# Fewer fills of the score tiles on GpSimd, and a later load of one small column

## The chip, the cores and the metric

The kernel runs on one core of a Trainium2 chip. The metric is the device time of one execution in microseconds; the median of three runs is used. The core has five engines that run their own instruction queues in order and wait for each other by semaphores: TensorE (PE; its weight loads are shown as PEld), VectorE (DVE), ScalarE (ACT), GpSimd (POOL) and SyncE (SP), which here only issues DMA transfers.

## The reference

Gated linear attention over 4 batches, 8 heads, 768 steps and a head width of 48, all in fp32, and then a normalised MLP block on rows of 8 x 48 = 384:

```python
for t in range(S):
    state = alpha[:, :, t, :, None] * state + np.einsum('bhd,bhe->bhde', k[:, :, t], v[:, :, t])
    y[:, :, t] = np.einsum('bhd,bhde->bhe', q[:, :, t], state)
x = y.transpose(0, 2, 1, 3).reshape(B, S, H * D)
...
xn = (x - mu) / np.sqrt(var + 1e-06) * g_ln
out = x + np.maximum(xn @ w_ch1, 0.0) @ w_ch2
```

`w_ch1` is 384 x 1536 and `w_ch2` 1536 x 384. Both reach the chip as 64-bit words and are turned into fp32 there.

## The kernel before

The 768 steps are cut into 6 chunks of 128 steps; a chunk of one batch is one call of the generator `attention(c, b)`. In a chunk the recurrence becomes products: cumulated logarithms of alpha (ACT `la` L293, PE `lps` L298 for chunk 0 and L525 later), their exponentials times q and k (ACT L303 and L304, DVE `qk` L312), transposes (`tps` L328, copied to `qT` and `kT` by L333 and L335), scores (`aps` L369), and then `yps`, which sums scores times v (L424). `ups` (L399) and the DVE product L408 carry the state on.

Chunk 0 (`whole`) is done as one block of 128 x 128 scores for each head: ACT copies the scores from PSUM to an SBUF tile `at` (L379), and POOL clears what lies on the wrong side of the diagonal by an affine select (L380). Two tiles `at` of 128 x 1024 serve four batches in turn, so the selects are four for the batches 0 and 1 and four for the batches 3 and 2. All later chunks are done in two halves of 64 steps, and there DVE writes the scores by a predicated copy (L383) that writes only the positions that count. It relies on zeros standing in the others. POOL therefore fills both tiles with zeros at the start (L278) and again when chunk 0 has read them for the last time (L462). A half of an `at` tile then holds the scores of a batch.

The normalised rows `xn` (DVE L479) are transposed (`xps` L490). For chunk 0, DVE multiplies them by the column `g_col` of g on the way to `xT` (L493); for the later chunks g is multiplied into the weights instead (ACT L782, first at 65.9 us). `g_col` is a slice of the tile `small`, of 128 x 3 elements, and is loaded by a DMA that POOL issues (L310). All other DMA transfers are issued by SP: the inputs (`ra`, `rq`, `rk`, `vn`; L143, L147, L149, L160), the rows that carry the gates (`row` L316, `gate` L389), and the weight pieces `ws` (L211).

A weight piece is unpacked from 64-bit words by DVE (L223, L225, L227), ACT (L229), and DVE again (L231, L233). The first piece lets the hidden products of chunk 0 start (`hps` L564 on PE).

The order on every engine is the order of the program's text, and that is written out by hand: `ORDER` is a string in which each letter advances one generator by one step (`a` to `x` the attention of one chunk and batch, `A` on the weight pieces, `0` to `3` the loads, `Y`, `Z`, `M` and `V` the MLP's products, and so on). Constants are made on POOL first, in the tile `consts`: the triangle `tri` (L176, L177), the identity (L179, L180), the masks of halves (L182, L185) and a bf16 identity of halves (L189).

Of the kernel before, what the change touches and what calls it, by code (L numbers as in the profile page):

```python
# [51 lines left out]
def kernel(  # L52
# [36 lines left out]
    nc = tc.nc  # L89
# [4 lines left out]
    P = 128  # L94
# [18 lines left out]
    HS = P // 2  # L113
# [79 lines left out]
    small = cpool.tile([P, NF + 2], FP32, name="small")  # L193
    g_col, eps, least = small[:, :NF], small[:, NF:NF + 1], small[:, NF + 1:NF + 2]
# [79 lines left out]


    ats = [cpool.tile([P, NP, 2, 2, HS], FP32, name=f"at{i}") for i in range(2)]
    for at in ats:
        nc.gpsimd.memset(at, 0.0)  # L278

    x_of, xT_of, hT_of, las, lps_of, qkT_of, aps_of, ob_of = ({} for _ in range(8))  # L280

# [2 lines left out]
    def attention(c, b):  # L284
# [20 lines left out]
        yield  # L305
        ends = slice(P - 1, P) if whole else slice(HS - 1, P, HS)
        ne = 1 if whole else 2
        if c == b == 0:
            with nc.allow_non_contiguous_dma(reason="one small column load"):
                nc.gpsimd.dma_start(g_col, g_ln.rearrange("(f p) -> p f", p=P))  # L310
        for n in (0, 1) if whole else (1, 0):
            nc.vector.tensor_mul(qk[:, n], raws.pop(("qk"[n], c, b)), (eq, lv)[n])  # L312
            if n == 0:
# [4 lines left out]
        at = ats[b % len(ats) if whole else 1 - b % 2]  # L318
        if not whole:
            at = at.rearrange("k p i s t -> k (p i s t)")[:, b // 2 * NP * P:][:, :NP * P].rearrange(  # L320
                "k (p s t) -> k p s t", s=2, t=HS)
# [54 lines left out]
        if whole:  # L376
            for i in range(2):
                to = at[:, :, i].rearrange("k p s t -> k p (s t)")
                nc.scalar.copy(out=to, in_=aps[i].rearrange("k p s t -> k p (s t)"))  # L379
                nc.gpsimd.affine_select(out=to, in_=to, compare_op=AOP.is_ge, fill=0.0, base=0,  # L380
                                        pattern=[[0, NP], [1, P]], channel_multiplier=-1)
        else:
            nc.vector.copy_predicated(  # L383
                out=at.rearrange("k p s t -> k (p s) t"),
                data=aps[0].rearrange("k p s t -> k (p s) t"),
                mask=mask_of_halves.unsqueeze(1).broadcast_to([P, 2 * NP, HS]))
# [72 lines left out]
                nc.vector.scalar_tensor_tensor(out=x, in0=yps[1], scalar=1.0, in1=x, op0=AOP.mult,  # L459
                                               op1=AOP.add, accum_out=mean)  # L460
        if whole and b + len(ats) >= B:
            nc.gpsimd.memset(at, 0.0)  # L462
        yield
        if not whole:
            x_of[c, b] = kept = dram.tile([P, DM], FP32, name="kept", tag="kept", bufs=4 * B)
# [467 lines left out]
    turns |= {"PQ"[h]: second_of_chunk_0(h) for h in range(2)}  # L933
    turns |= {"4": sums(), "5": scores()}
    turns |= {chr(ord("a") + n): attention(n // B, n % B) for n in range(NCB * B)}
    turns |= {chr(ord("A") + i): take_weights(i) for i in range(len(pieces))}
    turns |= {"M": mlp(), "V": hidden_products(NCB - 1), "S": combine_first(), "W": combine_weights(), "R": relus(),
# [34 lines left out]
```

## Time and profile before

| | |
|---|---|
| median of three runs | 423.36 us (423.02 to 423.86) |
| the profiled execution's own time | 425.22 us |
| its span on the core | 423.5 us |
| instructions in the profile | 14142 |
| granted TensorE clock | full speed in all slices |
| DMA | 43.95 MB, 104 GB/s mean over the span |

The profile is of one execution. Times in it are microseconds from the start of the span unless marked ns. A line such as `start us, us, engine line op out<-in` gives the start, the length, the engine, the line of the kernel, and in brackets how long the engine had been idle before and what ended that; `x4` merges four instructions of a kind. In the chain of work that ended last each step is what released the next one.

### The profile page before, as it was taken

The page shows a single profiled execution, that of the slowest core. Times are in us where ns is not written, and L with a number is a line of the kernel's source. Part 1 is how long each engine was busy: PE and PEld are TensorE (multiplying, and loading weights), DVE is VectorE, ACT ScalarE, POOL GpSimd, SP SyncE. Part 2 cuts the span into 40 slices and gives each one's busy share as a digit, 9 for nine tenths or more (in the row PEclk, how much of TensorE's full clock was granted, in tenths as well). Part 3 has the DMA queues.
Part 4 walks back from the last instruction along what each step waited for, and adds up shares of the span by engine and source line. Part 5 has one row for each costly group of instructions (what it writes and reads, how often), then busy time and mean ns, then how long its engine had stood idle before and what let it go on. Part 6 is the DMA issues. An engine that isn't in the chain of part 4 may idle for free.

```text
span 423.5 us, 14142 instructions
## 1 busy us (share of the span) xinstructions
PE 416.0 (98%) x5988; PEld 366.6 (87%) x5988; DVE 326.9 (77%) x626; ACT 228.0 (54%) x572; POOL 155.2 (37%) x182
## 2 busy tenths in 40 slices
PE   7989999999999999999999999999999999999996
PEld 5878878756778889998889998899998899988996
DVE  3689989898998989778668667749676588756684
ACT  6987577969535879434666066496432541124300
POOL 4242010200116391244671334670145650656414
PEclk9999999999999999999999999999999999999999
DMA  7879866774533341161503136002122000130001
GB/s 234 242 210 276 259 180 187 229 224 146 115 109 122 97 147 45 38 180 30 150 23 111 61 90 159 0 22 39 42 82 70 0 2 0 39 112 2 0 20 56
DMA packets 50791, 43.95 MB, mean 104 GB/s; under 512 B 23164, under 2 KB 46844, under 8 KB 50728
## 3 DMA queue, kind: packets, MB, share of 16 engines
q1 hardware_dynamic: 50696, 43.04, 35.3%
q8 instruction: 47, 0.77, 0.8%
q14 instruction: 16, 0.13, 0.1%
q0 software_dynamic: 32, 0.00, 0.0%
HBM read 34.29 MB, written 8.74 MB: 102 GB/s over the span
## 4 chain that ended last, share of the span: by engine, by line
PE 91%; DVE 3%; DMA 3%; ACT 1%; issue 1%; SPq 1%; DVEq 0%
PE ops L676 31%; PE hps L856 31%; PE ops L576 7%; PE hps L564 7%; PE yps L440 5%; PE aps L541 2%; PE ups L399 2%; PE tps L349 2%; DMA ws<-in_moe_w_ch_dram 2%; PE lps L525 1%; DMA ra<-in_alpha_dram 1%; DVE qk L312 1%; PE xps L506 1%; PE tps L328 1%; PE xps L490 1%
## 5 line engine op out<-in xcount | busy, mean ns | idle before, releaser
L692 POOL TENSOR_TENSOR ob<-ob,u 128x192 f32<-128x192 f32 x40 | 25.5, 648 | 88.5 <-DVE ob L689 66.1
L856 PE MATMUL hps<-sum,w 128*128 128x256 f32 x192 | 47.5, 382 | 0.1
L414 POOL TENSOR_TENSOR mid<-mid,gate 112x192 f32<-112x192 f32 x20 | 10.7, 536 | 92.3 <-DVE mid L412 55.2
L856 PEld LDWEIGHTS hps<-sum,w 128*128 128x128 f32 x192 | 36.1, 190 | 5.1 <-DVE qk L312 0.2
L676 PE MATMUL ops<-w,hT 128*128 128x192 f32 x224 | 39.9, 327 | 0.0
L676 PEld LDWEIGHTS ops<-w,hT 128*128 128x128 f32 x224 | 37.0, 190 | 0.3
L564 PE MATMUL hps<-xT,w 128*128 128x256 f32 x144 | 33.6, 385 | 1.1 <-DVE w L233 0.8
L856 PE MATMUL hps<-xT,w 128*128 128x256 f32 x136 | 34.4, 380 | 0.0
L564 PEld LDWEIGHTS hps<-xT,w 128*128 128x128 f32 x144 | 26.5, 190 | 6.6 <-issue 1.1
L576 PE MATMUL ops<-w,hT 128*128 128x384 f32 x96 | 32.0, 488 | 0.0
L907 ACT ACTIVATE hT<-hT 128x512 f32<-128x512 f32 x48 | 27.3, 629 | 7.8 <-POOL hT L894 2.7
L856 PEld LDWEIGHTS hps<-xT,w 128*128 128x128 f32 x136 | 25.8, 190 | 3.5
L676 PE MATMUL ops<-ws,sum 128*128 128x192 f32 x160 | 28.6, 327 | 0.0
L576 PEld LDWEIGHTS ops<-w,hT 128*128 128x128 f32 x96 | 17.9, 190 | 11.5
L686 DVE TENSOR_TENSOR ob<-ops,ob 128x192 f32<-128x192 f32 x50 | 17.0, 351 | 13.0 <-PE ops L676 7.6
L676 PEld LDWEIGHTS ops<-ws,sum 128*128 128x128 f32 x160 | 26.4, 190 | 0.0
L359 ACT COPY qT<-tps 112x512 uint16<-112x512 uint16 x32 | 17.2, 600 | 16.0 <-PE tps L349 16.0
L676 PE MATMUL ops<-ws,hT 128*128 128x192 f32 x128 | 23.4, 326 | 0.0
L510 ACT COPY xT<-xps 128x384 uint16<-128x384 uint16 x32 | 13.5, 491 | 16.9 <-PE xps L506 16.9
L676 PE MATMUL ops<-more,sum 128*128 128x192 f32 x120 | 22.2, 328 | 0.0
L676 PEld LDWEIGHTS ops<-ws,hT 128*128 128x128 f32 x128 | 21.3, 190 | 0.1
L440 PE MATMUL yps<-mid,qT 48*64 48x48 f32 x320 | 20.9, 220 | 0.0
(254 smaller groups left out, 1138.0 us busy)
## 6 DMA issues: line engine op xcount, KB each, us to landing
ws<-in_moe_w_ch_dram SPq DMA_DIRECT2D x12, 768.0 KB, 5.9
vn<-in_v_dram SPq DMA_DIRECT2D x12, 384.0 KB, 3.9
kept<-x SPq DMA_DIRECT2D x20, 192.0 KB, 2.7
ob<-kept SPq DMA_DIRECT2D x20, 192.0 KB, 2.2
out_dram<-ob SPq DMA_DIRECT2D x19, 192.0 KB, 1.9
rq<-in_q_dram SPq DMA_DIRECT2D x16, 192.0 KB, 4.1
rk<-in_k_dram SPq DMA_DIRECT2D x16, 192.0 KB, 4.3
ra<-in_alpha_dram SPq DMA_DIRECT2D x14, 192.0 KB, 2.5
```

What stands on the lines that cost most here:

```text
L349: nc.tensor.transpose(tv[cs, n, p, w], words[halves[h], n, p, i, :cs.stop - cs.start, w], ident_of_halves[halves[h]])
L359: nc.scalar.copy(out=to, in_=tps[h].bitcast(UINT16).rearrange("r (n p w t) -> r n p t w", n=2, p=NP, w=2)[:R, n])
L414: nc.gpsimd.tensor_mul(new, new, by)
L440: nc.tensor.matmul(yps[r][halves[s], i, p], of, by, start=not (odd and inner), stop=bool(inner or not odd), skip_group_check=bool(odd))
L510: nc.scalar.copy(out=xT_of[c][:, :, b, halves[h]].bitcast(UINT16).rearrange("r f (t w) -> r f t w", w=2), in_=xps[h].bitcast(UINT16)[:, :2 ...
L564: nc.tensor.matmul(hps, w1[:, j // 2, f, j % 2 * P:][:, :P], xT_of[0][:, f, bs], start=(f == 0), stop=(f == NF - 1))
L576: nc.tensor.matmul(ops_of[b], hT_of[c][:, j, b], w2[:, j], start=(j == 0), stop=(j == NJ - 1))
L676: nc.tensor.matmul(acc, lhs[:, j], rhs[:, j], start=(j == 0), stop=(j == NT - 1))
L686: nc.vector.tensor_add(x, acc, x)
L692: getattr(nc.gpsimd, f"tensor_{op}")(x, x, y)
L856: nc.tensor.matmul(acc[:, i], w, b, start=True, stop=True)
L907: nc.scalar.activation(out=x, in_=x, func=AFT.Relu)
```

## The change

Three edits, all in what POOL does in the first 30 us. The fills of both `at` tiles at the start go. The fill behind chunk 0 is limited to the rows 0 to 63 and the second half of the columns of each block, a quarter of the tile: the select of chunk 0 leaves zeros in all other positions that the later chunks rely on. The load of `g_col` moves from the middle of the first call of `attention` to behind the second select of batch 1. The quantity that is computed stays the same.

```diff
     ats = [cpool.tile([P, NP, 2, 2, HS], FP32, name=f"at{i}") for i in range(2)]
-    for at in ats:
-        nc.gpsimd.memset(at, 0.0)
...
         ne = 1 if whole else 2
-        if c == b == 0:
-            with nc.allow_non_contiguous_dma(reason="one small column load"):
-                nc.gpsimd.dma_start(g_col, g_ln.rearrange("(f p) -> p f", p=P))
...
                 nc.gpsimd.affine_select(out=to, in_=to, compare_op=AOP.is_ge, fill=0.0, base=0,
                                         pattern=[[0, NP], [1, P]], channel_multiplier=-1)
+            if b == 1:
+                with nc.allow_non_contiguous_dma(reason="one small column load"):
+                    nc.gpsimd.dma_start(g_col, g_ln.rearrange("(f p) -> p f", p=P))
...
         if whole and b + len(ats) >= B:
-            nc.gpsimd.memset(at, 0.0)
+            nc.gpsimd.memset(at[:HS, :, :, 1], 0.0)
```

In the built program POOL's order changes as written, and the two casts of L189 come to stand ahead of the two selects of L185. The order of the instructions on all other engines stays as it was. Two copies L379 of ACT no longer wait for POOL, and POOL's first select L380 waits for POOL's own earlier work as well.

## The prediction

> **What bounds the kernel now.** First the page: busy shares, and the chain of work that ended last.
>
> ```profile
> PE 416.0 (98%) x5988; PEld 366.6 (87%) x5988; DVE 326.9 (77%) x626; ACT 228.0 (54%) x572; POOL 155.2 (37%) x182
> ```
>
> TensorE is busy for 416.0 of 423.5 us and the chain runs 91% over it; POOL has 37% and no share of the chain. So work taken from POOL is worth something only where TensorE waits behind POOL, and all that the change touches lies in the first 30 us. There I read the chain in order of time.
>
> ```profile
> 15.79 0.36 DVE st L408
> ...
> 18.05 7.05 DMA ws<-in_moe_w_ch_dram
> ...
> 30.48 2.83 PE hps L564 x12
> ```
>
> The head runs: loads of alpha (landing to 6.23), the first scores and products on PE (11.09 to 15.76), the state on DVE, the issue of the first weight piece at 18.05, its landing at 25.10, its unpacking on DVE and ACT, and at 30.48 the first hidden products. What moves a step of this moves the end almost one for one. Next POOL alone, in order of time:
>
> ```profile
> 3.22 0.51 POOL L189 CAST consts<-consts 64x64 bf16<-64x64 f32 x2
> 3.79 0.95 POOL L278 MEMSET at<- 128x1024 f32 x1
> 4.68 0.94 POOL L310 DMA_DIRECT2D small<-in_moe_g_ln_dram  x1
> 12.98 2.39 POOL L380 TENSOR_SCALAR_AFFINE_SELECT at<-at 128x512 f32<-128x512 f32 x4 [7.36 <-ACT at L379]
> 21.87 2.67 POOL L380 TENSOR_SCALAR_AFFINE_SELECT at<-at 128x512 f32<-128x512 f32 x4 [6.49 <-ACT at L379]
> 27.29 1.88 POOL L462 MEMSET at<- 128x1024 f32 x2 [2.76 <-PE yps L424]
> ```
>
> The first column is the start, the second the length. POOL stands idle for 7.36 us ahead of the first four selects, for 6.49 us ahead of the next four, and 4.06 us after the last fills (L414 follows at 33.24). Then DVE, which reads what POOL makes:
>
> ```profile
> 9.79 0.55 DVE L312 TENSOR_TENSOR qk<-rk,lps 128x384 f32<-128x384 f32 x1 [0.86 <-DMA rk<-in_k_dram]
> ...
> 22.79 0.54 DVE L493 TENSOR_TENSOR xT<-xps,small 128x384 f32<-128x384 f32 x1
> 23.57 0.56 DVE L493 TENSOR_TENSOR xT<-xps,small 128x384 f32<-128x384 f32 x1 [0.24 <-PE xps L490]
> 25.12 0.56 DVE L223 TENSOR_SCALAR w<-ws 128x768 int32<-128x768 int32 x1 [1.00 <-DMA ws<-in_moe_w_ch_dram]
> ...
> 30.25 0.73 DVE L383 COPY_PREDICATED at<-consts,aps 128x512 f32<-128x512 int32 x1
> ```
>
> L493 is the first reader of the column of g, L383 the first reader of the fills behind chunk 0, L223 the start of the unpacking that carries the chain. Last the column's own load, from the view of its tile and from the queues between 4 and 11 us:
>
> ```profile
> DMA to landing us min/median/max: 5.4/5.4/5.4
> ```
>
> ```profile
> q0 software_dynamic: 32, 0.00, 0.6%
> ```
>
> Issued at 4.68, it landed 5.4 us later, at 10.1. Its 32 packets lie between 8 and 10 us and took 0.6% of 16 engines over 7 us: 0.67 us, or 0.04 us for each engine.
>
> **The change, part by part.** The sum is made against the profiled execution: span 423.5, own time 425.22, so 1.7 us around the span. That run is 1.86 us above the median of the runs (423.36); I carry the difference over to the median. About 0.2%, 0.85 us, is what a measurement of this kernel can tell from no change (the three runs spread over 0.84).
>
> *The two fills at the start.* Two of 0.95 us go. The built program then has the casts of L189 ahead of the selects of L185, and both end at about 1.67 + 0.15 + 0.51 + 0.52 = 2.9 instead of 3.73. Who waits for that? The trace puts 0.18 us of PE's wait ahead of its first product (3.93) down to L189, but the wait in the program is for POOL's third counted instruction, the select of L177, which ended at 1.5. And the product is early anyway: ACT runs its four logarithms before the first exponential, and the fourth starts at 6.25, when alpha lands. Bounds 0 and -0.18; I take 0, covered by that load.
>
> *Waits.* ACT's two copies L379 each lose a wait on POOL, and POOL's first L380 gains one on its own earlier work. The separate waits of L462 on POOL took 17 ns each; one less ahead of the copy, one more ahead of the select: 0, at most 0.03 either way. No other wait changes, and every other engine's order is the same.
>
> *The load of g leaves 4.68.* POOL is free 0.94 us earlier, with nothing to do before 12.98. On the DMA engines its 0.04 us apiece goes from the stretch in which DVE waits 0.86 us for the k of batch 1 (it reads at 9.79) and 0.43 us for a q at 12.21. The first matters: the copy of kT behind it releases the scores at 11.09. By the packets' own time the gain is 0.04; the bounds are 0 and both waits, 1.29. I take 0.04, the row of the load itself.
>
> *It comes back behind the select of batch 1*, at 12.98 + 2.39 = 15.37. Queued behind it on POOL are the selects at 21.87: 6.5 us of room for 0.94. SP's queue is untouched. Landing as before gives 15.37 + 5.4 = 20.8, against 22.79 for L493. What does lateness cost? Behind L493 on DVE stands L223, which waits for its weights until 25.12 anyway; two L493 of 0.55 must be through, so the column may land until 24.0, that is 8.6 us after issue. PE waits too: the transposes of the next chunk reuse a bank that L493 reads, but PE stands idle 0.85 us ahead of 30.48. For the bounds: a POOL instruction beside DVE took 1.15 instead of 0.51 (L414 at 39.13), +0.64, and the loads of 384 KB of q, the slowest near, took 7.8: 15.37 + 0.64 + 7.8 = 23.8, still in time. Its packets add 0.04 us to each engine while the chain's weights land: +0.04; at least 0. The nearest row is the load itself, so I take 20.8 and no stall.
>
> A rule that speaks against this move: the Trainium skill, "SBUF — State Buffer", section "A bandwidth-pool intuition that's wrong (but worth ruling out)", says that a load issued by GpSimd took about 3100 ns instead of 620 beside a VectorE copy, since the descriptors can't be written while VectorE holds the shared port. The trace bears out that the two hold each other up: L479 took 0.79 us beside the selects at 22.08 and 0.47 to 0.48 elsewhere. An estimate by that page, 2.5 us more, gives 23.3, and the sum would stay the same.
>
> *The fills behind chunk 0* shrink from 128x1024 to 64x512. Memsets of 128 and 1024 columns took 0.20 and 0.95, so 0.84 ns a column: 0.52 each. The second can't start before PE ends its yps (28.1), so the fills end near 28.7 instead of 29.17. L383 stands behind L233 on DVE and starts at 30.25: 1.08 us of cover before, 1.5 after. Even at the old price nothing changes. 0.
>
> Sum: 0 + 0 - 0.04 + 0.04 + 0 = 0. Forecast 423.4.
>
> **The rivals.** *The column stood in the way of the loads.* The DMA rate falls from 362 GB/s (8 to 9 us) to 274 and 220 in the next two, just where its packets are, and k lands at 9.77. If DVE's waits of 0.86 and 0.43 both vanish, the scores and all behind them come 1.29 us earlier: 422.1. Against it: 0.04 us per engine, and the weights' own landing, 7.05 us on engines 97% busy from 15 to 26 us, may give part of it back; half of it would be no change. Only one of the two waits is worth less than 0.85: after the first alone, q at 12.21 is next.
>
> *The column lands late (slower).* At 4.68 DVE was idle (2.74 to 7.19) while POOL issued; at 15.37 it is busy for most of the next 7 us, and the DMA engines have larger loads queued. It decides from 8.6 us after issue on. At twice the old landing, 10.8, it is there at 26.2; the two L493 end at 27.3, L223 starts 2.1 us late, and the first hidden products with it: 425.5. For it speaks only the 7.8 us of q; against it, that its packets go by a queue of their own and landed in 5.4 at 93% load.
>
> *The order of the loads slips.* A head bound by loads can fall out otherwise by as much as the runs differ, 0.84, and a bit more, to either side: 422.4 or 424.3.
>
> **How the numbers follow.** The forecast has 0.52. The loads set free have 0.24, the slip 0.06 to the faster side and 0.06 to the slower, the late column 0.12. So faster 0.30, same 0.52, slower 0.18. The range runs from 421.9, just below the freed loads, to 424.9, beyond the slower slip; left out are most of the late column and a little below, under 0.2. The forecast's own range is 422.5 to 424.2.
>
> **What would show it.** In the profile after: POOL without 128x1024 fills; the column issued near 15.4 and landing near 20.8; L493 at 22.8 with no wait on that load; fills of 0.5 us done before 29; L383 near 30.25, and the first hidden products at 30.5. Wrong would be: the k of batch 1 read well before 9.79 with the scores before 11 (freed loads), or a wait of L493 on the column and L223 after 25.1 (late column), or anything that starts after 31 us and is not a shift of the head.

## The result, and the profile after

The changed kernel took 424.46 us (median of 10 executions, 423.71 to 426.81), the kernel before 423.01 in as many beside it (422.67 to 423.86): a ratio of 1.0029, 95% interval 1.0017 to 1.0042. It is slower by 0.29%: small, but the interval leaves out no change, and it is above the 0.2% that the prediction took for the least that can be told from none. The ratios here are those of the recorded comparisons; the quotient of the medians beside them differs by up to 0.001 (here it is 1.0034). Two later comparisons of the same kernel gave 1.0013 [1.0000, 1.0025] and 1.0035 [1.0014, 1.0056]. Three of the changed kernel's 34 executions (426.81, 427.60 and 428.38) had a granted clock of 0.995 or 0.996 and the rest 0.999 or 1.000; without such executions, of either kernel, the medians of the three comparisons still lie 1.28, 0.59 and 1.10 us above the kernel before, so the clock doesn't carry the loss.

The profile was taken of an execution of 424.11 us with a span of 422.4; the one shown of before was 1.86 us above its median. So the two spans say nothing on which kernel is slower, and the steps have to be read one by one. The busy shares first, from the page:

```profile
PE 416.2 (99%) x5988; PEld 366.7 (87%) x5988; DVE 326.7 (77%) x626; ACT 227.9 (54%) x572; POOL 154.0 (36%) x180
```

POOL has two instructions and 1.2 us less; TensorE has as much to do as before. The chain of waits, in order of time (start, length, engine and line; most lines lie 2 to 5 lower than before; the column's load is now L379):

```profile
18.17 0.55 PE xps L488 x3
...
20.25 1.49 DVE qk L307 x3
21.74 0.72 DVE xn L477
...
29.32 2.83 PE hps L562 x12
```

In this execution the landing of the weights, 7.05 us of the chain shown of before, is not on the chain; it runs over products on TensorE and DVE's work instead. The first hidden products start at 29.32. POOL in order of time (last column: idle time before it and what ended it):

```profile
1.80 0.51 POOL L189 CAST consts<-consts 64x64 bf16<-64x64 f32 x2
...
12.61 2.40 POOL L375 TENSOR_SCALAR_AFFINE_SELECT at<-at 128x512 f32<-128x512 f32 x4 [9.72 <-ACT at L374]
14.95 0.94 POOL L379 DMA_DIRECT2D small<-in_moe_g_ln_dram  x1
21.45 2.67 POOL L375 TENSOR_SCALAR_AFFINE_SELECT at<-at 128x512 f32<-128x512 f32 x4 [5.56 <-ACT at L374]
26.87 0.52 POOL L460 MEMSET at<- 64x512 f32 x1 [2.75 <-PE yps L422]
27.80 0.52 POOL L460 MEMSET at<- 64x512 f32 x1 [0.41 <-PE yps L422]
```

The fills of 128x1024 are gone, the column is issued behind the first four selects, and the two small fills end at 28.3. Then DVE, and the landing of the column from the view of its tile:

```profile
22.37 0.54 DVE L491 TENSOR_TENSOR xT<-xps,small 128x384 f32<-128x384 f32 x1
23.15 0.56 DVE L491 TENSOR_TENSOR xT<-xps,small 128x384 f32<-128x384 f32 x1 [0.24 <-PE xps L488]
23.62 0.90 DVE L223 TENSOR_SCALAR w<-ws 128x768 int32<-128x768 int32 x1
...
29.09 0.72 DVE L381 COPY_PREDICATED at<-consts,aps 128x512 f32<-128x512 int32 x1
```

```profile
DMA to landing us min/median/max: 5.4/5.4/5.4
```

Issued at 14.95, the column landed at 20.4. Its first reader L491 starts at 22.37 without a wait, and the unpacking L223 has no wait for its weights either. Nothing in this head shows where more than 1 us goes. That question is what the experiments are for.

### The profile page after: what moved, and what is told of

Same layout as the page of the kernel before. It is cut to its first block, busy times and chain, and to the rows that moved or that the text cites. A ratio compares the mean times of both kernels' runs of the same rounds, so it can differ in the third digit from the quotient of the medians.

```text
span 422.4 us, 14139 instructions
## 1 busy us (share of the span) xinstructions
PE 416.2 (99%) x5988; PEld 366.7 (87%) x5988; DVE 326.7 (77%) x626; ACT 227.9 (54%) x572; POOL 154.0 (36%) x180
## 4 chain that ended last, share of the span: by engine, by line
PE 94%; DVE 3%; DMA 1%; issue 1%; ACT 1%; SPq 0%; DVEq 0%
PE ops L674 31%; PE hps L854 31%; PE ops L574 7%; PE hps L562 7%; PE yps L438 5%; PE aps L539 3%; PE ups L397 2%; PE tps L344 2%; PE tps L323 2%; PE lps L523 2%; DVE qk L307 1%; DMA ra<-in_alpha_dram 1%; PE yps L422 1%; PE xps L504 1%; PE xps L488 1%
## 5 line engine op out<-in xcount | busy, mean ns | idle before, releaser
L412 POOL TENSOR_TENSOR mid<-mid,gate 112x192 f32<-112x192 f32 x20 | 12.1, 608 | 89.8 <-DVE mid L410 55.1
```

The costliest lines, as they stand in the source:

```text
L412: nc.gpsimd.tensor_mul(new, new, by)
```

## The experiments

Three sets, each of four kernels on one chip beside the kernel before, which ran 35 times in each; every experiment ran 11 or 12 times. The expectations name theories. In the first set A is the moved load, B the missing fills, and C neither, only the luck of an execution. In the second, B is split: B1 is that POOL's being busy at the start counts, B2 that the score tiles and the waits on them count; D is that the time at which the column is loaded costs it (at once in fills_only, late in the changed kernel). In the last set B1 has a second condition: the time rises when POOL has no fills at the start while the column is loaded.

### The parts alone

**The column's load moved, the fills as before** (g_only):

```diff
-        if c == b == 0:
-            ... nc.gpsimd.dma_start(g_col, ...)
+            if b == 1:
+                ... nc.gpsimd.dma_start(g_col, ...)
```

> Before, with one part of the change: the load of the column of g stands behind the second select of batch 1 (issue near 15.4 us instead of 4.7); the fills stay as before. Theory A, the moved load carries the loss (it adds to the loads that land between 15 and 25 us, or its landing is awaited): about +1.2 us, as the whole change (+1.45 us of medians, ratio 1.0029), and in the profile either a wait of L493 on it or a later start of L223. Theory B, the fills carry it: 0, within 0.4 us. Theory C, no part carries it and the head only falls out otherwise (which load lands last): anything between -0.8 and +1.2 us with no wait on POOL or on the column.

Measured: 424.24 us, 1.0005 [0.9989, 1.0022]. The column landed 6.1 us after an issue at 14.85, and no reader waited for it. Theory A, which expected about +1.2 us, falls.

**The start fills gone and the quarter behind chunk 0, the column's load left in its place in the text** (fills_only):

```diff
-    for at in ats:
-        nc.gpsimd.memset(at, 0.0)
...
-            nc.gpsimd.memset(at, 0.0)
+            nc.gpsimd.memset(at[:HS, :, :, 1], 0.0)
```

> Before, with the other parts: no fills at the start and a quarter behind chunk 0; the load of the column of g stays in the text where it was. Without the fills POOL reaches it sooner, near 2 us, so that it now runs among the first loads. Theory A: 0, within 0.4 us, or up to 0.3 us worse if the column delays the loads of alpha. Theory B: about +1.2 us. Theory C: between -0.8 and +1.2 us.

Measured: 424.93 us, 1.0025 [1.0007, 1.0043], as B expected: without the fills the time rises with the column early, too. Here the profile shows a place for part of it. POOL in order of time, then ACT's logarithms in this kernel:

```profile
1.77 0.94 POOL L308 DMA_DIRECT2D small<-in_moe_g_ln_dram  x1
```

```profile
4.44 0.52 ACT L291 ACTIVATE la<-ra 128x384 f32<-128x384 f32 x1 [0.54 <-DMA ra<-in_alpha_dram]
6.66 0.99 ACT L291 ACTIVATE la<-ra 128x384 f32<-128x384 f32 x2 [1.69 <-DMA ra<-in_alpha_dram]
```

and ACT's in a second run of the program before (control, below):

```profile
5.16 0.52 ACT L293 ACTIVATE la<-ra 128x384 f32<-128x384 f32 x1 [0.83 <-DMA ra<-in_alpha_dram]
6.19 0.52 ACT L293 ACTIVATE la<-ra 128x384 f32<-128x384 f32 x1 [0.51 <-DMA ra<-in_alpha_dram]
```

The fills had kept the column's load back until 4.68. Without them it goes out at 1.77, while the loads of alpha, issued from 0.82, are still coming in. Between 2 and 8 us the column's 32 packets then take 3.4 us of the engines' time (3.5% of 16 engines over 6 us), and the other loads move 1.46 MB, against 1.68 in the kernel before. The third and fourth logarithm run back to back from 6.66 and end at 7.65, where those of the control end at 6.71: 0.94 us later, and the first hidden products follow at 29.96 against 29.09. The end at 7.65 is the latest of all profiled executions, the others lying between 6.37 and 7.08; the first hidden products are not, so this is a part of the loss at most. By this one profile the old fills also served as a spacer. The changed kernel avoids this by moving the load, and can't owe its loss to it. The two losses are of one size, though; whether a second cause is common to them is not shown.

**The quarter behind chunk 0 alone** (quarter_only):

```diff
-            nc.gpsimd.memset(at, 0.0)
+            nc.gpsimd.memset(at[:HS, :, :, 1], 0.0)
```

> Before, with the fills behind chunk 0 cut to a quarter and nothing else. All theories: 0, within 0.4 us, since L383 starts behind L233 on DVE over 1 us after the fills end. The program before 26 us is the same as before, so a larger difference than 0.4 us would show how much of a difference comes with any new program, whatever its text (theory C in its strongest form).

Measured: 423.87 us, 0.9990 [0.9975, 1.0005]: worth nothing.

**The program before again** (control; a comment is added):

> The kernel before with a comment added at its end: the same program. All theories: ratio 1.000, within 0.1%. It gives a second profile of the kernel before on this chip, to be set against the first (span 423.5): theory C expects that the landing of the first weights and the start of the first hidden products (30.48 in the first) differ by half a microsecond or more between two executions of the same program.

Measured: 423.79 us, 0.9991 [0.9977, 1.0005]. Two profiled executions of this one program differ by 1.39 us at the first hidden products (30.48 and 29.09) and by 1.2 us in span (423.5 and 422.3). A single profile is therefore no measure of a change of this size.

### What it takes to bring the loss about

**The changed kernel again** (after_again):

> The changed kernel once more, the same program, beside the three below on one chip. Theory B (the fills at the start carry it) and theory C (nothing does, the first runs of it were unlucky) part here: B expects 1.0029 again, within 0.0015; C expects 1.000 within 0.0015.

Measured: 424.35 us, 1.0013 [1.0000, 1.0025]: just outside what B expected, and inside C's range. The profiled execution was its fastest, 423.72.

**The same work at the start, on memory that nothing reads yet; column late** (fills_elsewhere_g_late). To the changed kernel are added two fills of 128x1024 into a part of the tile of `w_ch2` that is written much later. The order and the waits of all other engines stay those of the changed kernel.

```diff
     ats = [cpool.tile(...) for i in range(2)]
+    spare_w2 = w2.rearrange("p j m -> p (j m)")
+    for i in range(2):
+        nc.gpsimd.memset(spare_w2[:, 2560 + 1024 * i:][:, :1024], 0.0)
```

> The changed kernel plus two fills of 128x1024 on POOL at the start, into a part of the second weight's buffer that nothing uses until much later. POOL's order and times of the first 15 us are then those of before without its column load; no other engine's order or waits differ from the changed kernel. Theory B1 (what counts is that POOL is busy until 4.7 us, and the constants finished later): about as the moved load alone, 1.0005, so 1 us faster than the changed kernel. Theory B2 (what counts is the score tiles themselves, filled or not, with the waits that go with them): as the changed kernel, 1.0029. Theory C: 1.000 to 1.001 for this and the changed kernel alike.

Measured: 423.79 us, 0.9997 [0.9986, 1.0009]. The loss is gone with POOL busy at the start and the score tiles still unfilled: B2 falls. In this set the gap to the changed kernel, 0.56 us, is only just clear of nothing. Two smaller things on POOL come back with the fills: the casts of the identity stand behind the selects of the masks again, and the first select of chunk 0 loses its extra wait on POOL's own work. The kernel without the column, below, has both as the changed kernel has them and shows no loss, so they don't cost by themselves.

**The same with the column's load at its old place** (fills_elsewhere_g_early; the diff of g_only undone):

> The same two fills elsewhere, and the load of the column at its old place, so that it is issued near 4.7 us again: before in every time on POOL, but the score tiles aren't filled at first, and behind chunk 0 only by a quarter. Theory B1: 1.000 within 0.001. Theory B2: 1.0025 as the fills taken away alone. Theory D (the run without fills was slow because its column load was issued at 1.8 us, amid the loads of alpha, and the changed kernel because of its late column load): 1.000, and fills elsewhere with the late load as the changed kernel.

Measured: 423.64 us, 0.9995 [0.9982, 1.0007]: no loss either.

**The changed kernel without the column's load** (no_column):

```diff
+    nc.vector.memset(g_col, 1.0)
...
-            if b == 1:
-                ... nc.gpsimd.dma_start(g_col, ...)
```

> The changed kernel without the load of the column of g: VectorE fills the column with ones at the start, so g is left out of the result; nothing else differs. Theory D (the late load carries the loss): 1.000, 1.2 us faster than the changed kernel. Theories B1 and B2: as the changed kernel, 1.0029 within 0.0015. Theory C: as the changed kernel, both at 1.000 to 1.001.

Measured: 423.64 us, 0.9997 [0.9980, 1.0013]. Without the load the bare start costs nothing. B1 as it stood expected 1.0029 here and was wrong; the column was added to it after this run. D was right here and wrong with the fills elsewhere. Taken alone, this set fits C best, which expected 1.000 to 1.001 throughout.

### The three that decide, a second time

Missing fills without the column, and a late column with fills, were at 1.000; missing fills with a column were above it. A picture like that, with a theory fitted to it afterwards, can come from chance, so the last set repeats it on one chip.

**The changed kernel** (after_third):

> The changed kernel once more, beside three of its neighbours on one chip. Theory B1 (with no fills of GpSimd at the start and a column that is loaded, the time rises): 1.002 of before, about 424.4 us. Theory D (the column's late load alone): 1.001 to 1.002, and the same for the second runs of 'fills elsewhere, column late' and 'column moved alone'. Theory C (nothing but the luck of an execution: landings of the loads at the head, and the race of VectorE and GpSimd at 149 us): all four of this job within 0.0015 of each other.

**Fills elsewhere, column late** (fills_elsewhere_g_late_2):

> After with two fills of 128x1024 at the start that go to idle memory, the column late, a second time. Theory B1: 1.000 within 0.001, and 0.001 to 0.002 below after_third. Theory D: as after_third, about 1.0015. Theory C: within 0.0015 of after_third, either side.

**No column** (no_column_2):

> After without the load of the column of g (VectorE fills it with ones, so g is left out of the result), a second time. Theory B1: 1.000 within 0.001. Theory D: 1.000 within 0.001. Theory C: within 0.0015 of after_third, either side.

**Column moved alone** (g_only_2):

> Before with the load of the column moved behind the second select and the fills left as they were, a second time. Theory B1: 1.000 within 0.001. Theory D: as after_third, 1.001 to 1.002. Theory C: within 0.0015 of after_third, either side.

Measured, with the first runs beside them (the first of the last row is from the first set, on another chip):

| kernel | start fills | column | first: us, ratio | second: us, ratio |
|---|---|---|---|---|
| changed kernel | none | late | 424.35, 1.0013 [1.0000, 1.0025] | 424.83, 1.0035 [1.0014, 1.0056] |
| fills elsewhere | two, idle memory | late | 423.79, 0.9997 [0.9986, 1.0009] | 423.78, 0.9997 [0.9982, 1.0013] |
| no column | none | none | 423.64, 0.9997 [0.9980, 1.0013] | 423.58, 0.9997 [0.9980, 1.0014] |
| column moved alone | two, score tiles | late | 424.24, 1.0005 [0.9989, 1.0022] | 424.00, 1.0006 [0.9995, 1.0017] |

The changed kernel is 0.56 us above the one with fills elsewhere in the first comparison and 1.05 in the second; the mean of the two, 0.81, has an interval of 0.38 to 1.42 by resampling the executions. D expected the second and the fourth kernel to be as slow as the first, and they are not. C expected all four within 0.0015, and the first is 0.0029 to 0.0038 above the rest (0.0020 to 0.0030 by the medians). B1, in its new form, has its side of each comparison: 1.0035 where it said 1.002, and 1.000 for the others; the gap is larger than the 0.001 to 0.002 that it gave. What is shown is the condition: the time rises when POOL has no fills at the start and the column is loaded, late (1.0029, 1.0013, 1.0035) or in its old place in the text (1.0025, in one comparison), and either fills on any memory or the absence of the load brings it back. B1 names no mechanism, though, and the profiles were searched for one.

### Where in the execution

The column is not late in any of them. Its landing in the slowest case, from the tile's view of after_third:

```profile
DMA to landing us min/median/max: 6.4/6.4/6.4
```

From 14.69, it is there at 21.1; L491 reads it at 22.35 without a wait. In fills_elsewhere_g_late_2, which loses nothing, it took 6.3. Nor does the head end later: the first hidden products of the changed kernel start at 29.32, 29.82 and 29.50, those of fills_elsewhere_g_late at 29.94 and 29.49, of g_only at 30.15 and 29.85, of no_column at 28.94 and 30.32.

Laid over each other product by product, the profiles part at three later places. By 60 us the products have shifted by -0.5 to +1.4 us against those of fills_elsewhere_g_late_2, in kernels of either kind (the +1.4 is g_only's). Near 78 us DVE waits for a weight piece in two of the three profiles of the changed kernel, after_again and after_third, and in none of the six of its neighbours; here those two, and fills_elsewhere_g_late_2:

```profile
78.09 0.56 DVE L223 TENSOR_SCALAR w<-ws 128x768 int32<-128x768 int32 x1 [0.78 <-DMA ws<-in_moe_w_ch_dram]
```

```profile
78.25 0.56 DVE L223 TENSOR_SCALAR w<-ws 128x768 int32<-128x768 int32 x1 [0.72 <-DMA ws<-in_moe_w_ch_dram]
```

```profile
77.46 0.55 DVE L223 TENSOR_SCALAR w<-ws 128x768 int32<-128x768 int32 x1
```

The later products come 0.3 to 0.4 us later where it waits. But quarter_only, which loses nothing, has the same wait, 0.81 us. The third place is near 150 us. DVE and POOL in after_third, in order of time:

```profile
149.06 1.28 POOL L876 TENSOR_TENSOR hT<-hT,u 128x512 f32<-128x512 f32 x1
...
150.08 1.90 DVE L307 TENSOR_TENSOR qk<-rq,eq 128x384 f32<-128x384 f32 x1
150.29 1.27 POOL L879 TENSOR_TENSOR hT<-u 128x512 f32<-128x512 f32 x1
```

and in fills_elsewhere_g_late_2:

```profile
148.72 1.28 POOL L879 TENSOR_TENSOR hT<-hT,u 128x512 f32<-128x512 f32 x1
...
149.81 0.60 DVE L310 TENSOR_TENSOR qk<-rq,eq 128x384 f32<-128x384 f32 x1
149.95 1.60 POOL L882 TENSOR_TENSOR hT<-u 128x512 f32<-128x512 f32 x1
```

The same two instructions follow each other in both kernels. Either POOL's takes 1.60 and DVE's 0.60, or POOL's 1.27 and DVE's 1.90. In the second outcome DVE is 1.3 us late, and with it stands the chain of waits of after_third between 148 and 153 us:

```profile
149.62 2.36 DVE qk L307 x2
151.98 0.60 DVE hT L882
```

In fills_elsewhere_g_late_2 the chain stays on TensorE in that stretch and has nothing of DVE:

```profile
147.99 2.37 PE hps L857 x11
150.36 0.55 PE ups L400 x23
```

Every later product comes 0.75 to 0.85 us later where DVE loses, to the end. The Trainium skill, "SBUF — State Buffer", section "Who interferes with whom", says that a VectorE instruction with two inputs from SBUF contends with a GpSimd instruction that reads SBUF, and that the order of issue decides which of them blocks. Both are of these kinds, and in each outcome one of them has its short time and the other is longer. That the order decides can't be read here: DVE's instruction starts first in both outcomes, by 0.13 to 0.14 us in the nine profiles in which it takes 0.6 and by 0.17 to 0.23 in the five in which it takes 1.9. No experiment here separated them on purpose.

| profiled execution | first hidden products | span | from there to the end | DVE's `qk` near 150 us |
|---|---|---|---|---|
| before / control | 30.48 / 29.09 | 423.5 / 422.3 | 393.0 / 393.2 | 1.88 / 1.85 |
| changed kernel, three | 29.32 / 29.82 / 29.50 | 422.4 / 422.0 / 423.0 | 393.1 / 392.2 / 393.5 | 1.94 / 0.60 / 1.90 |
| fills elsewhere, late, two | 29.94 / 29.49 | 422.1 / 421.9 | 392.2 / 392.4 | 0.58 / 0.60 |
| no column, two | 28.94 / 30.32 | 421.7 / 422.1 | 392.8 / 391.8 | 0.60 / 0.60 |
| column moved, two | 30.15 / 29.85 | 423.9 / 422.6 | 393.8 / 392.8 | 0.60 / 0.60 |

The race is lost by DVE in two of three profiles of the changed kernel and in none of six of the neighbours in this table, which would be 0.5 of the 0.8 us. Outside the table it is lost in fills_only, the other kernel with a loss. This doesn't settle the matter: the kernel before lost it in both of its profiles, and its time is not above the neighbours'. The profiled executions of the changed kernel (424.11, 423.72 and 424.70) also lie in the faster half of its executions; those above, up to 428.38, are in no trace. So the place of the loss stays open. The late weight piece and this race are the candidates that have a price: each profile of the changed kernel has at least one of them, none of the six neighbours' has either, but the kernels before and quarter_only have one, too, and are not slower.

## Why the prediction was right or wrong

The time, 424.46, lies in the range (421.9 to 424.9), but the likeliest case was no change, at 423.4, and the kernel is slower by 0.29%, a case that had 0.18. That the range holds the time is luck: its upper end was put beyond a slip of the loads at the head, and the runs show no later head as the cause. By its steps:

- **Fills at the start: 0, bounds 0 and -0.18. This is the step that failed.** That nothing waits for POOL there held: the casts came at 1.80, and ACT's fourth logarithm, at 6.50 when alpha landed, was still the cover. The bounds excluded a loss, though: the prediction asked only who waits for POOL. The runs give +0.8 us [0.4, 1.4] for taking that work away while the column comes late (changed kernel against fills elsewhere); by what way stays open. With the load at its old place in the text it costs as much (1.0025), and part of that may come by a way that I had not listed: the load moves forward among the loads of alpha, and the logarithms end 0.94 us later.
- **Waits: 0.** Held, as far as the runs part them. With the fills elsewhere, ACT's copies have the waits of the changed kernel, and the ratio is 0.9997 twice; without the column POOL's select has its extra wait as well, and the ratio is 0.9997 twice.
- **The load leaves 4.68: -0.04, and comes back at 15.37: +0.04.** Held in sum: the move alone gave 1.0005 and 1.0006, both intervals with 1 inside. The issue came at 14.95, the landing at 20.4, L491 at 22.37, each within 0.5 us of its step. The prediction's remark that DVE's work might hold up the issue did not show: the issue took 0.94 as before, and the landing 5.4 to 6.4 in seven executions with a late column, far from 2.5 us more and from the 8.6 at which it would have begun to cost.
- **Fills behind chunk 0: 0.52 each, done near 28.7, worth 0.** Held: 0.52 each, done at 28.3, and 0.9990 alone.
- **Rivals.** The freed loads (422.1) did not come: the load moved alone shows no gain, whatever DVE waited for. The falling DMA rate that spoke for them was misread: 13 of the column's 32 packets lie between 8 and 9 us, at 362 GB/s, 19 between 9 and 10, at 274, and none between 10 and 11, where the rate is lowest, 220. The late column (425.5) was the wrong mechanism on the right side: slower, but with the column in place 2 us before its reader. The slip of the loads (0.84 to either side) was taken for rare, 0.12, and is as large as 1.39 us at the first hidden products between two executions of one program.

The sum treated edits as terms that add. Here the missing fills cost nothing without the column's load and 0.13 to 0.35% with it.

## What to carry to other kernels

An instruction that nobody waits for can still be a spacer: before deleting it, look at what moves forward on its queue, the DMA issues above all, and what is landing at that moment. When a part costs, measure it with and without the other parts, since its price can hang on one of them, and put equal work elsewhere before blaming the data that the deleted work wrote. A theory that is reworded to fit a run needs a further run. For an effect of a few tenths of a per cent compare many executions with repeats; one profile of each kernel differs by more.

## What the runs showed of the hardware

- One program, two executions: 1.39 us apart at the first hidden products, 0.7 of it by 11 us, in a stretch where the waits end on loads.
- The outcome of a race between a DVE and a POOL instruction, 0.60 and 1.60 us or 1.90 and 1.27, is not fixed by the program: the changed kernel shows both. It shifts the end by 0.75 to 0.85 us of 423.
- A load of 128x3 elements issued by POOL took 5.1 to 6.4 us to land in all these heads, though its 32 packets hold 1.5 KB: 5.1 when issued at 1.77, 5.4 at 4.68 (four executions), 5.4 to 6.4 near 15 us, beside the weights.
